# Reordering the prologue of an mLSTM + mixture-of-experts kernel: chunk 0's decays spread by fp32 products, two scans and a split moved

## The chip, the cores and the metric

The kernel runs on one core of one Trainium2 chip. The metric is the device time of one execution in microseconds (us), the median of three. A core has TensorE (PE in the rows; PEld is its weight load), VectorE (DVE), ScalarE (ACT), GpSimd (POOL) and SyncE (SP), which here only issues DMAs. Each engine takes its instructions in the order in which they were written; an instruction that has to wait holds back everything behind it on its engine.

## The reference

Two stages. The first is an mLSTM recurrence for 2 batches x 8 heads over 768 steps with head size 40:

```python
m_new  = max(f_gate + m, i_gate)
f_stab = exp(f_gate + m - m_new);  i_stab = exp(i_gate - m_new);  m = m_new
C = f_stab * C + i_stab * outer(v, k);   n = f_stab * n + i_stab * k
y[t] = sigmoid(o_gate) * (C @ q) / max(|n . q|, 1)
```

The second takes the 1536 tokens x of 320 numbers through all of four experts and adds them up with normalised weights p:

```python
out += p[:, e] * (relu(x @ w1[e]) @ w2[e])      # w1: 320 x 1024, w2: 1024 x 320
```

## The kernel before

The recurrence is computed in 12 chunks of 128 steps (`NCH`), six for each batch. For chunk n these helpers are called, each a few instructions:

- `spread(n)` copies the row of decays of each of the 8 heads to all 128 partitions, by 8 matrix products whose stationary operand is one column of a selector, broadcast (tile `fb`, in PSUM). `decay(n)` scans each of them against an identity on VectorE into a 128 x 128 matrix of products of decays (tile `dd`).
- `scores(n)` is k·q per head (tile `s`), `weigh(n)` multiplies it by `dd` (tile `pm`), `values(n)` scales v by the input gate (tile `vp`: a product on GpSimd and one column on ScalarE), `keys(n)` scales k (tile `kp`, GpSimd).
- `intra(n)` is pm·vp (tile `y`); `inter(n)` is q times the carried state (also a tile `y`), scaled on ScalarE into `yb`; `state(n)` makes the chunk's own state from kp and vp (tile `st`) and adds it to the decayed old one (tile `cs`); `carry(n)` decays the old state on GpSimd (tile `cd`).
- `norm(n)` divides and gates on VectorE (tile `xr`). `turn(n)` transposes `xr` on TensorE (tile `px`) and ScalarE writes the rounded part of x (tile `xst`); `turn_lo(n)` writes the remainder on VectorE.

The gates of the chunks of all 16 (batch, head) pairs are handled together, in two groups: columns of chunks 0 and 1 first, chunks 2 to 5 later (`(0, 2)` and `(2, NC)`). `gate_max` scans the running maximum, `gate_f` and `gate_i` make the decays `fs` and the input gates, `gate_starts` puts zeros at chunk starts, `gate_pair` splits the decays into two fp32r parts (tile `fr`) that `spread` reads, `gate_b` scans the running decays (VectorE, L248) and ScalarE copies them into `ib` (L252), `gate_t` transposes `ib` (tile `pit`, then `ibT`, L273), `gate_last` and `gate_l` make the per-chunk decay `bl` of the state.

The experts work on x and w1 in fp32r parts: `split_hi` on ScalarE rounds (tile `w1s`, L86), `split_lo` on GpSimd subtracts (L89). Expert 0's w1 is split in four quarters of 256 hidden columns (`quarter_hi`, `quarter_lo`). Expert 0 runs by `steps(k)` between the chunks: one step makes 256 hidden columns for 256 tokens in 16 products (tile `ph`, L128). The first step needs x of chunks 0 and 1 and quarter 0, the second needs quarter 1. Experts 1 to 3 follow when the recurrence is done.

All of this is under `manual_schedule`: the order of the calls is the order on every engine. Lines 489 to 583 are the prologue, written out by hand: the first DMAs, the gates, chunks 0 and 1, and the start of chunk 2. From line 595 a loop goes over chunks 2 to 11. `keep_warm(n)` is a product of zeros of n columns that fills a wait of TensorE (tile `pwm`). Tiles named `ph` and `po` take turns in two PSUM buffers each, and so do the tiles of `ps_w` and `ps_y`.

The lines that the prediction's steps touch, in the prologue of before:

```python
        gate_starts(0, 2, nc.vector)
        gate_pair(0, 2, nc.vector)
        gate_b(0, 2)
        gate_max(2, NC)
        spread(0, ps_h, "ph")
...
        norm(0)
...
        gate_b(2, NC)
        intra(1)
        norm(1)
...
        quarter_hi(1)
        gate_last(2, NC)
        quarter_lo(1)
```

Of the kernel before, what the change touches and what calls it, by code (L numbers as in the profile page):

```python
# [18 lines left out]
L = 128  # L19
# [22 lines left out]
def tile_mlstm_moe(ctx, tc, gt, qk, vk, ot, dp, w1, w2, out):  # L42
# [21 lines left out]
    def keep_warm(n, pool=ps_h, tag="ph"):  # L64

        pwm = pool.tile([L, n], F32, tag=tag, name="pwm")
        nc.tensor.matmul(pwm, zero[:, 0:L], zero[:, 0:n], start=True, stop=True)
# [96 lines left out]
    with ExitStack() as actx:  # L164
# [17 lines left out]
        def load_w1(half):  # L182
            f = slice(half * FF // 2, (half + 1) * FF // 2)
            wa = hps[0].tile([L, 2, FF // 2], F32, tag="h", name="wa")
            nc.sync.dma_start(wa, w1[0, :, 0:2, f])
            wb = hps[0].tile([L, 2, FF // 2], F32, tag="h", name="wb")
            nc.sync.dma_start(wb[:, 0], w1[0, :, 2, f])
            for i in range(2):
                w1r[2 * half + i] = wa[:, :, i * G:(i + 1) * G], wb[:, 0, i * G:(i + 1) * G]
# [9 lines left out]
        BH = B * H  # L199
        gat = gp.tile([BH, 2, S], F32, name="gat")  # L200
        mb = gp.tile([BH, S + 1], F32, name="mb")
        fs = gp.tile([BH, S], F32, name="fs")
        bs = gp.tile([BH, NC, L], F32, name="bs")

        ib = gp.tile([48, S], F32, name="ib")
# [15 lines left out]
        def gate_max(c0, c1):  # L221
            g = slice(c0 * L, c1 * L)
            nc.vector.tensor_tensor_scan(
                out=mb[:, c0 * L + 1:c1 * L + 1], data0=gat[:, 0, g], data1=gat[:, 1, g],
                initial=-1e30 if c0 == 0 else mb[:, c0 * L:c0 * L + 1],
                op0=ALU.add, op1=ALU.max,
            )
# [7 lines left out]
        def gate_starts(c0, c1, eng):  # L235

            eng.tensor_copy(bs[:, c0:c1, 0:1], fc[:, c0:c1, 0:1])
            eng.memset(fc[:, c0:c1, 0:1], 0.0)
# [15 lines left out]
        def gate_pair(c0, c1, eng):  # L254

            g = slice(c0 * L, c1 * L)
            eng.tensor_copy(fr[0:BH, g], fs[:, g])
            eng.tensor_sub(fr[32:32 + BH, g], fs[:, g], fr[0:BH, g].bitcast(F32))
# [18 lines left out]
        def gate_last(c0, c1):  # L277
            n, m = c1 - c0, B * NP
            last = lasts[c0] = gp.tile([BH, m, n], F32, tag=f"last{c0}", name="last")
            nc.gpsimd.tensor_mul(  # L280
                last, pair.unsqueeze(2).to_broadcast([BH, m, n]),
                gat[:, 0].rearrange("p (c t) -> p c t", t=L)[:, c0:c1, L - 1].unsqueeze(1)
                .to_broadcast([BH, m, n]),
            )
# [42 lines left out]
        def gate_o(j):  # L327
            og = acc[:, 2 * j:2 * j + 2]
            nc.scalar.activation(og, og, AF.Sigmoid)
# [4 lines left out]
        def spread(n, pool, tag):  # L334

            b, c = n // NC, n % NC
            fbs[n] = [pool.tile([L, 4, L], F32, tag=tag, name="fb") for _ in range(2)]
            for h in range(H):
                nc.tensor.matmul(
                    fbs[n][h // 4][:, h % 4, :],  # L340
                    sel[:, b * H + h:b * H + h + 1].to_broadcast([48, L]),
                    fr[:, c * L:(c + 1) * L], start=True, stop=True,
                )

        def load_f(n):
# [31 lines left out]
        def scores(n, pool=ps_w, tag="w"):  # L377
            ss[n] = [pool.tile([L, NP, L], F32, tag=tag, name="s") for _ in range(2)]
            qg, kg = qT(n), kT(n)
            for p in range(NP):  # L380
                for r in range(2):
                    q = slice(64 * r, 64 + D * r)
                    nc.tensor.matmul(ss[n][r][:, p, :], kg[q, p], qg[q, p], start=True, stop=True)  # L383
# [115 lines left out]
            load_vk(1, c)  # L499
        load_o(1)  # L500
        load_w1(1)
        make_identity(nc, ident)
        nc.gpsimd.memset(ib, 0.0)
        for t in vp + kp:
# [16 lines left out]
        gate_f(0, 2, nc.vector)  # L521
        gate_i(0, 2, nc.vector)
        gate_starts(0, 2, nc.vector)
        gate_pair(0, 2, nc.vector)
        gate_b(0, 2)
        gate_max(2, NC)
        spread(0, ps_h, "ph")
        scores(0)
        spread(1, ps_o, "po")
        gate_o(0)  # L530
        gate_last(0, 2)
        gate_f(2, NC, nc.gpsimd)
        gate_t(0, 2)
        keep_warm(512, ps_y, "y")
        decay(0)
        values(0)
        keys(0)
        weigh(0)
        scores(1, ps_h, "ph")
        gate_l(0, 2)  # L540
        gate_i(2, NC, nc.gpsimd)
        decay(1)
        intra(0)
        state(0, ps_w, "w")
        values(1)
        keys(1)
        weigh(1)
        keep_warm(256, ps_w, "w")
        inter(1, ps_w, "w")
        norm(0)  # L550
        gate_starts(2, NC, nc.gpsimd)
        gate_pair(2, NPE, nc.gpsimd)
        nc.sync.dma_start(f_d, fs)
        w2r = raws.tile([L, NF, DM], F32, tag="raw", name="w2r")
        nc.sync.dma_start(w2r, w2[0])
        carry(1)
        quarter_hi(0)
        quarter_lo(0)
        gate_b(2, NC)
        intra(1)  # L560
        norm(1)
        turn(0, ps_h, "ph")
        turn_lo(0)
        spread(2, ps_o, "po")
        keep_warm(256, ps_w, "w")
        turn(1, ps_h, "ph")
        turn_lo(1)
        scores(2)
        state(1)
        quarter_hi(1)  # L570
        gate_last(2, NC)
        quarter_lo(1)
# [174 lines left out]
```

## Time and profile before

| What | Value |
|---|---|
| Median of 3 runs | 430.84 us (430.82 to 430.94) |
| The profiled execution's own time | 431.67 us |
| Its span in the trace | 428.8 us |
| TensorE busy | 421.1 us (98%) |
| VectorE busy | 180.1 us (42%) |
| ScalarE busy | 125.7 us (29%) |
| GpSimd busy | 82.3 us (19%) |
| Granted TensorE clock | 1.00 in every stretch of 10 us |

Times in the rows are us from the start of the span. A timeline row gives the start, the length, the engine, the line, the operation, the tile written and the tiles read, and how many instructions stand together; in brackets the engine's idle time before it and what ended that. An fp32 product stands as two records on TensorE, an fp32r product or a transpose as one; a record's length holds the time in which the result runs out of the array, so that records overlap.

### The profile page before, as it was taken

The page shows a single profiled execution, that of the slowest core. Times are in us where ns is not written, and L with a number is a line of the kernel's source. Part 1 is how long each engine was busy: PE and PEld are TensorE (multiplying, and loading weights), DVE is VectorE, ACT ScalarE, POOL GpSimd, SP SyncE. Part 2 cuts the span into 40 slices and gives each one's busy share as a digit, 9 for nine tenths or more (in the row PEclk, how much of TensorE's full clock was granted, in tenths as well). Part 3 has the DMA queues.
Part 4 walks back from the last instruction along what each step waited for, and adds up shares of the span by engine and source line. Part 5 has one row for each costly group of instructions (what it writes and reads, how often), then busy time and mean ns, then how long its engine had stood idle before and what let it go on. Part 6 is the DMA issues. An engine that isn't in the chain of part 4 may idle for free.

```text
span 428.8 us, 6587 instructions
## 1 busy us (share of the span) xinstructions
PE 421.1 (98%) x2754; PEld 386.2 (90%) x2754; DVE 180.1 (42%) x321; ACT 125.7 (29%) x298; POOL 82.3 (19%) x94
## 2 busy tenths in 40 slices
PE   8999999999999999999999999999999999999997
PEld 5799899999998998898898998988989989889896
DVE  8869947574766321513313224223132242231321
ACT  5666233334324252403403114025031140120210
POOL 6854601220210260300710002007100010000000
PEclk9999999999999999999999999999999999999999
DMA  7985716347100011300110003001200000001001
GB/s 209 281 276 159 197 51 166 104 111 256 53 2 2 0 52 72 139 11 0 61 63 0 2 0 148 0 2 40 85 0 2 0 0 32 31 2 46 18 15 46
DMA packets 15077, 29.29 MB, mean 68 GB/s; under 512 B 1000, under 2 KB 10728, under 8 KB 13736
## 3 DMA queue, kind: packets, MB, share of 16 engines
q1 hardware_dynamic: 15048, 28.88, 21.9%
q8 instruction: 21, 0.34, 0.3%
q14 instruction: 8, 0.07, 0.1%
HBM read 26.86 MB, written 2.02 MB: 67 GB/s over the span
## 4 chain that ended last, share of the span: by engine, by line
PE 91%; DVE 4%; DMA 2%; issue 1%; ACT 1%; SPq 0%; POOL 0%; DVEq 0%
PE ph L128 41%; PE po L149 13%; PE po L150 13%; PE po L151 13%; PE y L445 5%; PE s L383 2%; PE y L431 2%; PE st L398 2%; DMA acc<-in_ot 2%; PE px L471 1%; DVE y L457 0%; DVE xr L461 0%; DVE w2s L89 0%; DVE xr L464 0%; DVE dd L356 0%
## 5 line engine op out<-in xcount | busy, mean ns | idle before, releaser
L128 PE MATMUL ph<-xst,w1s 128*128 128x512 f32 (+1 forms) x960 | 184.5, 350 | 0.0
L128 PEld LDWEIGHTS ph<-xst,w1s 128*128 128x128 f32 x960 | 154.8, 189 | 25.0
L137 ACT ACTIVATE h<-ph 128x512 fp32r<-128x512 f32 x96 | 57.4, 598 | 214.0 <-PE ph L128 213.9
L149 PE MATMUL po<-w2s,h 128*128 128x320 f32 x384 | 119.5, 311 | 0.0
L150 PE MATMUL po<-w2s,h 128*128 128x320 f32 x384 | 118.6, 309 | 0.0
L151 PE MATMUL po<-w2s,h 128*128 128x320 f32 x384 | 118.6, 309 | 0.0
L138 DVE SCALAR_TENSOR_TENSOR h<-ph,h 128x512 fp32r<-128x512 f32 x96 | 66.2, 690 | 121.4 <-ACT h L137 121.4
L149 PEld LDWEIGHTS po<-w2s,h 128*128 128x128 f32 x384 | 72.1, 188 | 0.9
L150 PEld LDWEIGHTS po<-w2s,h 128*128 128x128 f32 x384 | 72.1, 188 | 0.4
L151 PEld LDWEIGHTS po<-w2s,h 128*128 128x128 f32 x384 | 72.1, 188 | 0.0
L156 DVE SCALAR_TENSOR_TENSOR acc<-po,pw,acc 128x320 f32<-128x320 f32 x36 | 19.8, 551 | 100.0 <-PE po L151 100.0
L89 POOL TENSOR_TENSOR w1s<-raw,w1s 128x512 fp32r<-128x512 f32 (+1 forms) x24 | 23.6, 1011 | 62.4 <-ACT w1s L86 62.4
L356 DVE TENSOR_TENSOR_SCAN dd<-fb,id 128x512 f32<-128x512 f32 x24 | 29.3, 1264 | 0.2
L89 POOL TENSOR_TENSOR w2s<-raw,w2s 128x640 fp32r<-128x640 f32 x6 | 9.4, 1569 | 104.1 <-ACT w2s L86 104.1
L445 PE MATMUL y<-vp,pm 128*128 128x64 f32 x192 | 23.1, 273 | 1.2 <-DVE xst L479 0.9
L445 PEld LDWEIGHTS y<-vp,pm 128*128 128x128 f32 x192 | 22.5, 192 | 1.6 <-issue 1.1
L154 ACT ACTIVATE acc<-po,pw 128x320 f32<-128x320 f32 x12 | 6.3, 528 | 43.7 <-PE po L151 43.7
L438 ACT ACTIVATE yb<-y,ibT 128x41 f32<-128x41 f32 x80 | 16.0, 312 | 4.1 <-PE y L431 4.1
L389 DVE TENSOR_TENSOR pm<-s,dd 128x512 f32<-128x512 f32 x24 | 15.4, 683 | 0.5 <-PE s L383 0.3
L372 POOL TENSOR_TENSOR kp<-vk,dd 128x320 f32<-128x320 f32 x10 | 7.4, 736 | 36.6 <-DVE dd L356 36.6
L383 PE MATMUL s<-qk 64*128 64x128 f32 (+1 forms) x192 | 14.1, 284 | 0.0
L383 PEld LDWEIGHTS s<-qk 64*128 64x128 f32 (+1 forms) x192 | 11.8, 187 | 1.9 <-DVE dd L356 0.8
(89 smaller groups left out, 222.0 us busy)
## 6 DMA issues: line engine op xcount, KB each, us to landing
raw<-in_w SPq DMA_DIRECT2D x3, 1536.0 KB, 6.3
fb<-f_d SPq DMA_DIRECT2D x8, 512.0 KB, 7.5
raw<-in_w SPq DMA_DIRECT2D x3, 1280.0 KB
qk<-in_qk SPq DMA_DIRECT2D x4, 832.0 KB
vk<-in_vk SPq DMA_DIRECT2D x4, 640.0 KB, 8.1
acc<-in_ot SPq DMA_DIRECT2D x6, 320.0 KB, 10.8
out<-acc SPq DMA_DIRECT2D x12, 160.0 KB, 1.8
qk<-in_qk SPq DMA_DIRECT2D x4, 416.0 KB
```

Source lines behind the costliest of these rows:

```text
L89: eng.tensor_sub(lo, raw, hi.bitcast(F32))
L128: nc.tensor.matmul(ph[:, i, :], self.w1s[:, wi, f * L:(f + 1) * L], xst[:, xi, self.t0:self.t0 + n], start=(k == 0), stop=(k == len(TERMS) ...
L137: nc.scalar.activation(hh, ph, AF.Relu)
L138: nc.vector.scalar_tensor_tensor(out=hl, in0=ph, scalar=0.0, in1=hh.bitcast(F32), op0=ALU.max, op1=ALU.subtract)
L149: nc.tensor.matmul(po, hh[:, sl], ws[:, LO, f, :], start=(f == 0), stop=False)
L150: nc.tensor.matmul(po, hh[:, sl], ws[:, HI, f, :], start=False, stop=False)
L151: nc.tensor.matmul(po, hl[:, sl], ws[:, HI, f, :], start=False, stop=(f == NF - 1))
L156: nc.vector.scalar_tensor_tensor(out=acc[:, i, :], in0=po, scalar=pw[:, i, e:e + 1], in1=acc[:, i, :], op0=ALU.mult, op1=ALU.add,)
L356: nc.vector.tensor_tensor_scan(out=dds[n][:, 4 * i:4 * i + 4].rearrange("p h t -> p (h t)"), data0=fbs[n][i].rearrange("p h t -> p (h t)") ...
L383: nc.tensor.matmul(ss[n][r][:, p, :], kg[q, p], qg[q, p], start=True, stop=True)
L438: nc.scalar.activation(yb[:, h], y1[:, h, 0:D + 1], AF.Copy, scale=ibT[:, c, i:i + 1])
L445: nc.tensor.matmul(y[:, h, :], pms[n][:, h, :], vvs[n][:, h, :], start=True, stop=True)
```

## The change

Six things are edited, all in the prologue.

- The decays `fs` get a tile of 128 partitions (`fsw`), whose first 128 columns are cleared by a new memset on VectorE. Chunk 0's `spread` reads it directly, as fp32 products over 128 rows with a column of the identity. The other chunks read `fr` as before.
- `gate_pair` for chunk 0 goes; for chunk 1 it moves from VectorE to GpSimd.
- `gate_t(0, 2)`, and with it the copy to `ibT`, stands before the sigmoid of the output gates and the exponential of the later decays.
- `state(0)` stands before `intra(0)`, `values(1)` before the input gates of chunks 2 to 5, `intra(1)` before `norm(0)`, and `carry(1)` before the later `gate_starts` and `gate_pair`.
- `gate_b(2, NC)` moves from between `norm(0)` and `norm(1)` to behind `state(1)`.
- `scores(2)` stands before `turn(1)`, `spread(2)` behind it, and of the three `keep_warm` calls of this stretch one is left, in front of `turn(1)`.

```diff
-        fs = gp.tile([BH, S], F32, name="fs")
+        fsw = gp.tile([L, S], F32, name="fsw")
+        fs = fsw[0:BH]
...
-                    sel[:, b * H + h:b * H + h + 1].to_broadcast([48, L]),
-                    fr[:, c * L:(c + 1) * L], start=True, stop=True,
+                    ident[:, h:h + 1].to_broadcast([L, L]) if n == 0
+                    else sel[:, b * H + h:b * H + h + 1].to_broadcast([48, L]),
+                    (fsw if n == 0 else fr)[:, c * L:(c + 1) * L], start=True, stop=True,
...
+        nc.vector.memset(fsw[:, 0:L], 0.0)
...
-        gate_pair(0, 2, nc.vector)
         gate_b(0, 2)
         gate_max(2, NC)
+        gate_pair(1, 2, nc.gpsimd)
         spread(0, ps_h, "ph")
+        gate_t(0, 2)
         scores(0)
         spread(1, ps_o, "po")
+        gate_last(0, 2)
         gate_o(0)
-        gate_last(0, 2)
+        decay(0)
         gate_f(2, NC, nc.gpsimd)
-        gate_t(0, 2)
-        keep_warm(512, ps_y, "y")
-        decay(0)
...
+        decay(1)
+        values(1)
         gate_i(2, NC, nc.gpsimd)
-        decay(1)
+        state(0, ps_w, "w")
         intra(0)
-        state(0, ps_w, "w")
-        values(1)
...
-        keep_warm(256, ps_w, "w")
         inter(1, ps_w, "w")
+        intra(1)
         norm(0)
+        carry(1)
...
-        carry(1)
         quarter_hi(0)
         quarter_lo(0)
-        gate_b(2, NC)
-        intra(1)
         norm(1)
         turn(0, ps_h, "ph")
         turn_lo(0)
-        spread(2, ps_o, "po")
-        keep_warm(256, ps_w, "w")
+        scores(2)
+        keep_warm(256, ps_o, "po")
         turn(1, ps_h, "ph")
         turn_lo(1)
-        scores(2)
+        spread(2, ps_o, "po")
         state(1)
+        gate_b(2, NC)
         quarter_hi(1)
         gate_last(2, NC)
         quarter_lo(1)
```

What this does to the order on the engines is shown at three places. On ScalarE, early in the prologue, before: L273 is the copy to `ibT`, L329 the sigmoid, the second table load and L233 the exponential of the later decays, L368 the column of `vp`, L74 the copy of the first state.

```order
L252 ACTIVATE ib<-gat 16x256
L329 ACT_TABLE_LOAD
L329 ACTIVATE acc<-acc 128x640
L233 ACT_TABLE_LOAD
L233 ACTIVATE fs<-fs 16x512
L273 ACTIVATE ibT<-pit 128x96
L368 ACTIVATE vp_124<-ibT 128x8
L295 ACTIVATE bl<-pit 128x16
L243 ACTIVATE ib<-ib 16x512
L74 ACTIVATE cs_129<-st 64x4x64
```

The same place on ScalarE in the changed kernel, whose lines are two or three higher:

```order
L254 ACTIVATE ib<-gat 16x256
L275 ACTIVATE ibT<-pit 128x96
L331 ACT_TABLE_LOAD
L331 ACTIVATE acc<-acc 128x640
L235 ACT_TABLE_LOAD
L235 ACTIVATE fsw<-fsw 16x512
L371 ACTIVATE vp_124<-ibT 128x8
L297 ACTIVATE bl<-pit 128x16
L371 ACTIVATE vp_125<-ibT 128x8
L245 ACTIVATE ib<-ib 16x512
L74 ACTIVATE cs_129<-st 64x4x64
```

The copy to `ibT` moved ahead of both table loads; the column of `vp` stayed behind them, and the second chunk's column went ahead of the exponential of the later input gates.

On VectorE, around the end of chunk 1, before: L248 is the scan of the later running decays, L457 to L464 are `norm(1)`, L478 and L479 the remainders of x, L413 the sum of the state, L356 the decay scans of chunk 2.

```order
L464 TENSOR_TENSOR xr<-xr,y_254 128x320
L248 SCALAR_TENSOR_TENSOR gat<-fs,bs 16x512
L457 TENSOR_TENSOR y_314<-y_314,yb 128x8x41
...
L478 TENSOR_TENSOR xst<-px,xst 128x2x128
L479 TENSOR_TENSOR xst<-px,xst 64x128
L413 TENSOR_TENSOR cs_128<-cd,st 64x4x64
L413 TENSOR_TENSOR cs_128<-cd,st 40x4x41
L356 SCALAR_TENSOR_TENSOR dd<-fb,id_117 128x512 x2
```

The same place on VectorE in the changed kernel:

```order
L467 TENSOR_TENSOR xr<-xr,y_262 128x320
L460 TENSOR_TENSOR y_289<-y_289,yb 128x8x41
...
L481 TENSOR_TENSOR xst<-px,xst 128x2x128
L482 TENSOR_TENSOR xst<-px,xst 64x128
L416 TENSOR_TENSOR cs_128<-cd,st 64x4x64
L416 TENSOR_TENSOR cs_128<-cd,st 40x4x41
L250 SCALAR_TENSOR_TENSOR gat<-fsw,bs 16x512
L359 SCALAR_TENSOR_TENSOR dd<-fb,id_117 128x512 x2
```

The scan now stands behind both additions of the state of chunk 1.

On ScalarE, what follows that scan, before: L252 copies it into `ib`, L473 and L474 write x, L86 rounds quarter 1 of w1, then the next sigmoid with its table load and the first evacuation of an expert's step.

```order
L252 ACTIVATE ib<-gat 16x512
L473 ACTIVATE xst<-px 128x2x128
L474 ACTIVATE xst<-px 64x128
L473 ACTIVATE xst<-px 128x2x128
L474 ACTIVATE xst<-px 64x128
L86 ACTIVATE w1s_91<-wa 128x2x256
L86 ACTIVATE w1s_91<-wb 128x256
L329 ACT_TABLE_LOAD
L329 ACTIVATE acc<-acc 128x640
L137 ACTIVATE h<-ph 128x512
```

The same place in the changed kernel:

```order
L476 ACTIVATE xst<-px 128x2x128
L477 ACTIVATE xst<-px 64x128
L476 ACTIVATE xst<-px 128x2x128
L477 ACTIVATE xst<-px 64x128
L254 ACTIVATE ib<-gat 16x512
L86 ACTIVATE w1s_91<-wa 128x2x256
L86 ACTIVATE w1s_91<-wb 128x256
L331 ACT_TABLE_LOAD
L331 ACTIVATE acc<-acc 128x640
L137 ACTIVATE h<-ph 128x512
```

The copy of the running decays went behind x of both chunks, and stands directly ahead of the rounding of quarter 1 of w1.

## Rows read from the trace of the kernel before

**Rows 1.** The first line of the page: the span.

```profile
span 428.8 us, 6587 instructions
```

**Rows 2.** The chain of waits that ended last, from chunk 2 to the transposes of chunk 3; columns: start, us, engine, tile, line.

```profile
31.65 1.77 PE y L445 x14
...
34.30 0.41 DVE cs L413
...
48.48 0.50 DVE xr L464
...
49.11 0.52 PE px L471 x3
```

**Rows 3.** The timeline of VectorE in the prologue and at chunk 4's decays (start us, us, engine, line, operation, out<-in, idle before).

```profile
0.94 0.48 DVE L507 MEMSET fr<- 48x512 f32 x1
...
5.68 0.06 DVE L238 MEMSET fs<- 16x2 f32 x1
...
6.54 0.68 DVE L248 TENSOR_TENSOR_SCAN gat<-fs,bs 16x256 f32<-16x256 f32 x1
7.14 1.25 DVE L223 TENSOR_TENSOR_SCAN mb<-gat,mb 16x512 f32<-16x512 f32 x1
8.32 2.30 DVE L356 TENSOR_TENSOR_SCAN dd<-fb,id 128x512 f32<-128x512 f32 x2
...
17.03 1.33 DVE L248 TENSOR_TENSOR_SCAN gat<-fs,bs 16x512 f32<-16x512 f32 x1
19.24 0.51 DVE L457 TENSOR_TENSOR y<-y,yb 128x328 f32<-128x328 f32 x1 [0.88 <-PE y L445]
...
24.04 0.76 DVE L413 TENSOR_TENSOR cs<-cd,st 64x256 f32<-64x256 f32 x2 [0.76 <-PE st L398]
24.81 2.34 DVE L356 TENSOR_TENSOR_SCAN dd<-fb,id 128x512 f32<-128x512 f32 x2
...
30.31 1.28 DVE L389 TENSOR_TENSOR pm<-s,dd 128x512 f32<-128x512 f32 x2
...
41.94 3.67 DVE L356 TENSOR_TENSOR_SCAN dd<-fb,id 128x512 f32<-128x512 f32 x2
```

**Rows 4.** The timeline of TensorE in the prologue, same columns.

```profile
6.65 0.96 PE L339 MATMUL fb<-fr,sel 48*128 48x128 f32 x7 [0.71 <-DVE fr L258]
...
12.69 2.00 PE L445 MATMUL y<-vp,pm 128*128 128x64 f32 x16 [0.22 <-POOL vp L367]
14.52 0.93 PE L398 MATMUL st<-vp,kp 128*104 128x105 f32 x8
...
16.24 1.16 PE L431 MATMUL y<-cs,qk 104*128 104x128 f32 x8 [0.33 <-ACT cs L74]
...
21.38 0.55 PE L471 MATMUL px<-ident,xr 128*128 128x128 f32 x3 [0.26 <-DVE xr L464]
...
23.70 2.15 PE L128 MATMUL ph<-xst,w1s 128*128 128x256 f32 x16
25.78 1.09 PE L269 MATMUL pit<-ident,ib 48*128 48x48 f32 x8
26.80 2.18 PE L128 MATMUL ph<-xst,w1s 128*128 128x256 f32 x16
```

**Rows 5.** The timeline of ScalarE in the prologue, same columns.

```profile
7.68 1.28 ACT L329 ACT_TABLE_LOAD   x1
9.02 0.74 ACT L329 ACTIVATE acc<-acc 128x640 f32<-128x640 f32 x1
...
11.07 0.63 ACT L233 ACTIVATE fs<-fs 16x512 f32<-16x512 f32 x1
11.61 0.22 ACT L273 ACTIVATE ibT<-pit 128x96 f32<-128x96 f32 x1
...
15.49 0.70 ACT L74 ACTIVATE cs<-st 64x256 f32<-64x256 f32 x2 [0.46 <-PE st L398]
...
19.88 0.63 ACT L252 ACTIVATE ib<-gat 16x512 f32<-16x512 f32 x1
...
22.40 0.62 ACT L86 ACTIVATE w1s<-wa 128x512 fp32r<-128x512 f32 x1
...
29.07 0.60 ACT L137 ACTIVATE h<-ph 128x512 fp32r<-128x512 f32 x1 [1.59 <-PE ph L128]
```

**Rows 6.** The timeline of GpSimd in the prologue and at chunk 4's decays, same columns.

```profile
7.30 1.10 POOL L280 TENSOR_TENSOR last<-pair,gat 16x16 f32<-16x16 f32 x1 [2.45 <-DVE gat L248]
...
9.82 1.08 POOL L232 TENSOR_TENSOR fs<-fs,mb 16x512 f32<-16x512 f32 x1
11.91 0.72 POOL L367 TENSOR_TENSOR vp<-vk,ibT 128x320 f32<-128x320 f32 x1 [1.01 <-ACT ibT L273]
12.59 0.74 POOL L372 TENSOR_TENSOR kp<-vk,dd 128x320 f32<-128x320 f32 x1
13.28 1.08 POOL L242 TENSOR_TENSOR ib<-gat,mb 16x512 f32<-16x512 f32 x1
...
21.55 0.25 POOL L280 TENSOR_TENSOR last<-pair,gat 16x32 f32<-16x32 f32 x1
23.10 1.27 POOL L89 TENSOR_TENSOR w1s<-wa,w1s 128x512 fp32r<-128x512 f32 x1 [1.30 <-ACT w1s L86]
...
42.98 3.98 POOL L89 TENSOR_TENSOR w2s<-w2r,w2s 128x640 fp32r<-128x640 f32 x2 [4.98 <-ACT w2s L86]
```

## The prediction

> **What bounds the kernel now.** I read the page first: a span of 428.8 us [rows 1], TensorE busy for 98% of it. That alone would say that only TensorE's own work counts, so I then read the chain of waits for the stretch behind the prologue. From 34.30, where the state of chunk 2 is added, to 48.98, where `norm(3)` ends, its pieces are VectorE's, one behind the other; TensorE takes over at 49.11 with the transposes of chunk 3 and keeps the chain from there [rows 2]. So the prologue counts through one event only: when VectorE can start that run at 34.30. It starts after `st` of chunk 2, which stands on TensorE behind `intra(2)`, whose second product starts at 31.65 [rows 2], just after the two `pm` of chunk 2 (30.31 + 1.28 = 31.59) [rows 3]. These stand behind the remainder of the second expert step, which waits for ScalarE's h at 29.07, which waits for TensorE's second step [rows 5], begun at 26.80 [rows 4]. Whatever moves the second step's end moves the end of the kernel by as much.
>
> Then the timelines, engine by engine. Up to the transposes of chunk 1 at 21.38 TensorE waits for others four times [rows 4]; from 23.70 to the second step's start at 26.80 it goes without a wait [rows 4]. What the second step needs was early: quarter 1 of w1 was there at 23.10 + 1.27 = 24.37 [rows 6], and the copy of the running decays for `pit` at 19.88 + 0.63 [rows 5].
>
> **The head, up to the transposes of chunk 1.** The new memset has 128 columns; one of 512 took 0.48, one of 16x2 took 0.06 [rows 3]. I take 0.2, between them. `gate_pair` leaves VectorE: from the end of the memset at 5.74 to the scan at 6.54 [rows 3] 0.80 goes, less the 0.04 that remain. Net, VectorE's scans come about 0.55 earlier: `gate_b` at 5.98, `gate_max` at 6.6, `dd` at 7.75 instead of 8.32.
>
> TensorE can start the spread at 6.1 instead of 6.65. The fp32 form gives 16 records. Sixteen fp32 records of 64 columns over 128 rows took 1.83 from start to next start (12.69 to 14.52); eight of 128 columns took 1.16 with the run-out, so twice that, 2.32, is the upper end [rows 4]. I take 1.83, since the record's own pace was the same in both. It ends at 7.93; `pit` follows (half of 1.09, [rows 4]), and `ibT` is copied at 8.5 to 8.75.
>
> Here the ScalarE order bites. Before, the first table load started at 7.68 and `ibT` came last, at 11.61 [rows 5]. Now the loads start at 8.75: 1.28 + 0.74 + 1.28 + 0.63 [rows 5] lead to 12.7, and the `vp` column behind them (I give it the 0.22 of `ibT`) to 12.9. Chunk 0's first `st` cannot start before that; before, the product in this place started at 12.69 [rows 4]. So hoisting `ibT` gains nothing at this point and loses 0.25. The two switches go by the rows: from the sigmoid's end (9.76) to the exponential (11.07) is 1.31, load included [rows 5]. The Trainium skill (ScalarE: Activation LUTs, What ACT_TABLE_LOAD costs) gives an additional drain of about 1.38 us for a switch, 2.66 in all; by that the `vp` column would come some 2.8 later and the sum below would be near +3.5, but the trace shows no such drain, and the measurement decides.
>
> `st` (0.8, its 0.93 without the run-out) and `y` (1.83) then occupy TensorE to 15.6. `inter(1)` needs the state's copy on ScalarE, which stands behind the exponential of the later input gates, which waits for GpSimd. GpSimd now has the pair of chunk 1, two small instructions, ready at 6.0, just when VectorE starts `gate_b` and then `gate_max`. The row of `last` shows what such a meeting costs: 1.10 at 7.30, against 0.25 at 21.55 for one of twice the size, ending as `gate_max` ended (8.39) [rows 3, 6]. So I let the pair finish at 8.4 and `last` at 8.7, 0.3 later than before. From there 2.5 to the end of the second `fs` instruction (8.40 to 10.90), then `vp`, `kp`, `vp` and the later input gates, 0.72 + 0.74 + 0.72 + 1.08 [rows 6], end at 14.4; exponential and copy, 0.63 + 0.70 [rows 5], give 15.7. `inter(1)` starts at 15.7 instead of 16.24, 0.55 earlier. The fp32 products' upper end would put `y`'s end and `inter(1)` at 16.1, 0.15 earlier; without the meeting 15.6, 0.65 earlier. That the meeting is a full block is also the Trainium skill's rule (SBUF — State Buffer, Who interferes with whom): a VectorE instruction with two inputs in SBUF and a GpSimd instruction that reads SBUF exclude each other, and the later one waits to the end. The `last` row agrees with it.
>
> From `inter(1)` everything to the transposes is TensorE, ScalarE and VectorE in the same sequence; `norm(0)` ends about 17.2, and since the scan at 17.03 (1.33, [rows 3]) has gone from its back, `norm(1)` waits for TensorE alone, as before (0.88 idle at 19.24, [rows 3]). So the transposes of chunk 1 come at 21.38 - 0.55 = 20.8. Behind them the order has `spread(2)` where `scores(2)` was: both eight products of about 1 us, a draw. First expert step: 23.70 - 0.55 = 23.15; VectorE's addition of the state: 24.04 - 0.55 = 23.5.
>
> **The late scan.** Here the order takes it back. The addition ends its turn after 0.77 (24.04 to 24.81, [rows 3]), at 24.25. Then `gate_b(2, NC)`: 1.33 [rows 3], to 25.6. ScalarE has stood at its copy since x of chunk 1 and everything behind waits too: copy 0.63, to 26.25; rounding quarter 1, 0.62 [rows 5], to 26.8 (they overlap by a little). GpSimd subtracts: 1.27 [rows 6], to 28.1. On TensorE the first step ends its turn 2.08 after its start (23.70 to 25.78, [rows 4]), at 25.2, and `pit` waits for the copy until 26.3, a new wait of 1.05; `pit` takes 1.02 (25.78 to 26.80), the second step's first product goes at 27.3, and its second needs GpSimd's remainder and starts at 28.1, a new wait of 0.6. Before, that second product followed directly behind 26.80, at about 27.0. The step ends 1.1 later than before: that is the sum, -0.55 for the head and +1.65 for the late scan.
>
> Then h at 30.2, `pm` of chunk 2 at 31.4, the addition at 35.4 instead of 34.30, and VectorE's run to the transposes, which come at 50.2. The new waits on VectorE's side have no cover, as rows 2 show; TensorE's spare time before 49.11 only grows. SP's queue: the store of the decays and the weights behind it start about 1 us later, since `carry(1)` stands ahead of them on GpSimd; what they bring is used from 38 on, so I cost that at nothing. The left-out warm-up products cost nothing as long as the granted clock stays at 1.00.
>
> Against the profiled execution: 431.67 + 1.1 = 432.8. The runs' median is 430.84, 0.83 below it; the difference is carried over: 431.9.
>
> **The rivals.**
> *The late scan is covered.* If the second step does not in fact wait for the copy, the rounding and the remainder, the head's gain goes through: 430.84 - 0.55 = 430.3. For it: TensorE is 98% busy and before it never waited there. Against it: the new order on ScalarE, and 1.33 + 0.63 + 0.62 + 1.27 behind an addition that itself stands behind TensorE's `st`.
>
> *The meeting at chunk 4 goes the other way.* The second scan of chunk 4's decays meets the two `w2s` instructions of GpSimd: the two scans took 3.67 at 41.94 where two undisturbed ones took 2.34, and GpSimd began at 42.98 [rows 3, 6], just before the second scan (41.94 and half of 2.34 is 43.1). If GpSimd comes 0.1 to 0.2 later in relation to VectorE, the scan is first, and 3.67 - 2.34 = 1.33 of VectorE's run goes: +1.1 - 1.33, 430.6, not slower. Both sides hang on `st` and `intra` of chunk 2 and should move alike, but the margin is small. It decides from the point where the second scan starts ahead of GpSimd.
>
> *The fp32 products run at the lower clock.* Left-out warm-ups and new waits of about a microsecond on TensorE could let the granted clock fall from 2.4 to 1.2 GHz. The spread would take up to twice 1.83, and the head some 1.3 to 2 more than I have: about 433.5. Against it: the wait of 0.71 at 6.65 [rows 4] left the clock at 1.00.
>
> **How the numbers follow.** Forecast as worked out: 0.57. Late scan covered: 0.12. Chunk 4 the other way: 0.20. Lower clock or another added wait: 0.11. A measurement of this kernel tells 0.2% from no change, that is 0.86 us: slower means above 431.70, faster below 429.98. The forecast's own range is 431.2 (head at its best, and 0.4 for overlaps that I added as if in series) to 432.6 (fp32 upper end); three quarters of it, 0.43, lie above 431.70, 0.14 inside. Chunk 4: 0.15 inside, 0.05 faster. Covered: 0.07 inside, 0.05 faster. Lower clock: 0.11 slower. Together: faster 0.10, same 0.36, slower 0.54. The range reaches down to the two rivals on the other side and up to the fp32 bound: 430.1 to 432.7.
>
> **What would show it.** In the profile of the changed kernel: `dd` of chunk 0 near 7.75; the first `st` near 12.9, released by ScalarE's `vp` column; the transposes of chunk 1 near 20.8; the scan of the later decays near 24.3; a wait of TensorE of about 1.05 before `pit`, released by ScalarE, and a second of 0.6 in the second step, released by GpSimd; the transposes of chunk 3 near 50.2. I am wrong if the second expert step starts before 26.8 without a wait, if the scans of chunk 4 take 2.3 instead of 3.7, or if the granted clock leaves 1.00.

## The result and the profile after

| | before | changed |
|---|---|---|
| Median, both measured together | 430.89 us | 442.31 us |
| Its executions | 430.82, 430.84, 430.94, 433.81 | 434.05, 439.99, 444.63, 445.33 |
| Granted TensorE clock, mean of each of these executions of the changed kernel | | 0.992, 0.977, 0.961, 0.965 |
| Profiled execution | 431.67 (span 428.8) | 445.33 (span 443.5) |

The changed kernel is slower: by the medians 442.31 - 430.89 = 11.4 us, and the ratio is 1.0133 with an interval of 1.0083 to 1.0182. Every ratio in this document leaves out executions more than 1.5% above the fastest of their kernel, here the two above 444 us, which are the same effect at a larger size, as the clock beside each time shows. So this ratio rests on two executions only. The forecast was 431.9 within 430.1 to 432.7: the sign came out, the size did not.

The first thing to look at is the clock. The page's first line, the share of the engines and the row of the granted clock, in tenths over 40 slices of the span:

```profile
span 443.5 us, 6596 instructions
...
PE 435.0 (98%) x2758; PEld 399.9 (90%) x2758; DVE 179.9 (41%) x320; ACT 125.2 (28%) x298; POOL 82.5 (19%) x96
...
PEclk9658799999999999999999999999999999999999
```

TensorE is busy for 98% as before, and for 435.0 us instead of 421.1. A busy share tells nothing of how fast the work went. The clock row does: slices two to five are at 5 to 8, where before had 9 throughout. Cut into stretches at the places where the clock changes (length, then busy time of PE, PEld, DVE, ACT and POOL, the granted clock, the DMA share, GB/s):

```profile
13.30:33.80 20.50, 19.68 (x96) 18.31 (x97) 8.26 (x21) 5.58 (x21) 5.52 (x9) 0.50 0.54 175
33.80:37.20 3.40, 2.62 (x20) 2.16 (x18) 2.92 (x3) 2.74 (x4) 1.67 (x3) 1.00 0.36 101
37.20:40.60 3.40, 3.40 (x16) 3.18 (x16) 0.69 (x1) 1.77 (x5) 1.96 (x3) 0.50 1.01 256
40.60:44.00 3.40, 3.38 (x28) 3.13 (x27) 2.66 (x4) 2.38 (x9) 2.53 (x3) 1.00 1.00 259
44.00:50.85 6.85, 6.85 (x41) 6.44 (x41) 4.66 (x11) 1.65 (x7) 4.74 (x6) 0.50 0.37 118
50.85:440.00 389.15, 386.91 (x2497) 358.73 (x2495) 148.82 (x260) 104.07 (x244) 54.88 (x54) 1.00 0.16 50
```

1.00 is 2.4 GHz and 0.50 is 1.2 GHz. The clock was at the lower level for 20.5 + 3.4 + 6.85 = 30.75 us. At half speed that can cost up to half of it, 15.4; the span is 443.5 - 428.8 = 14.7 longer than before's. The transposes of chunk 3 come behind all of this; they are the first of these rows (the second, the scans of chunk 4's decays, is used further down):

```profile
63.76 0.52 PE L474 MATMUL px<-ident,xr 128*128 128x128 f32 x3 [0.94 <-DVE xr L467]
56.54 3.70 DVE L359 TENSOR_TENSOR_SCAN dd<-fb,id 128x512 f32<-128x512 f32 x2
```

The transposes are 63.76 - 49.11 = 14.65 later than in before [rows 2], so behind them nothing more is lost. The experiment that holds the clock up, below, puts 12.2 of the 14.7 down to the falls.

What happened at the falls stands in the timeline of TensorE, which answers to [rows 4]:

```profile
0.78 6.50 PE L67 MATMUL pwm<-const-float32-0.0 128*128 128x512 f32 x8 [0.78 <-PEq L730]
7.12 1.95 PE L341 MATMUL fb<-fsw,ident 128*128 128x128 f32 x16
...
14.12 1.70 PE L401 MATMUL st<-vp,kp 128*104 128x105 f32 x8 [1.42 <-POOL ib L244]
15.61 3.55 PE L448 MATMUL y<-vp,pm 128*128 128x64 f32 x16
...
31.97 2.95 PE L128 MATMUL ph<-xst,w1s 128*128 128x256 f32 x16
35.10 1.09 PE L271 MATMUL pit<-ident,ib 48*128 48x48 f32 x8 [0.18 <-ACT ib L254]
...
37.11 3.51 PE L128 MATMUL ph<-xst,w1s 128*128 128x256 f32 x15 [0.60 <-POOL w1s L89]
```

The first fall, at 13.3, lies inside the wait of 1.42 ahead of chunk 0's `st`. From there the products take nearly twice as long: `y` 3.55 against 2.00 [rows 4]. The second, at 37.2, follows the wait of 0.60 in the second expert step. The third, at 44.0, follows no wait: TensorE was busy for 3.38 of the 3.40 us before it. The first rows also show that the spread started at 7.12, behind warm-up products that ran until 7.28.

VectorE, ScalarE and GpSimd, which answer to [rows 3], [rows 5] and [rows 6], in this order:

```profile
5.92 0.68 DVE L250 TENSOR_TENSOR_SCAN gat<-fsw,bs 16x256 f32<-16x256 f32 x1
6.53 1.25 DVE L225 TENSOR_TENSOR_SCAN mb<-gat,mb 16x512 f32<-16x512 f32 x1
8.21 2.34 DVE L359 TENSOR_TENSOR_SCAN dd<-fb,id 128x512 f32<-128x512 f32 x2 [0.43 <-PE fb L341]
```

```profile
9.68 0.25 ACT L275 ACTIVATE ibT<-pit 128x96 f32<-128x96 f32 x1 [2.63 <-PE pit L271]
9.95 1.28 ACT L331 ACT_TABLE_LOAD   x1
11.24 0.74 ACT L331 ACTIVATE acc<-acc 128x640 f32<-128x640 f32 x1
11.99 1.28 ACT L235 ACT_TABLE_LOAD   x1
13.29 0.63 ACT L235 ACTIVATE fsw<-fsw 16x512 f32<-16x512 f32 x1
13.83 0.20 ACT L371 ACTIVATE vp<-ibT 128x8 f32<-128x8 f32 x1
```

```profile
6.03 0.66 POOL L259 CAST fr<-fsw 16x128 fp32r<-16x128 f32 x1 [1.17 <-ACT ib L245]
6.77 1.25 POOL L260 TENSOR_TENSOR fr<-fsw,fr 16x128 fp32r<-16x128 f32 x1
...
12.71 1.08 POOL L244 TENSOR_TENSOR ib<-gat,mb 16x512 f32<-16x512 f32 x1
```

GpSimd's two small instructions took 0.66 and 1.25 while VectorE's two scans stood beside them; the same two on twice the columns took 0.39 and 0.71 at 18.01 and 18.48 of this trace, while VectorE was idle. The wait of 1.42 is put down to GpSimd's `ib`, which ended at 12.71 + 1.08 = 13.79; ScalarE's `vp` column at 13.83 + 0.20 = 14.03 came later, behind the two table loads, and `st` reads that column and not `ib`. That is the release that the prediction named, 1.2 us later than it said.

### The profile page after: what moved, and what is told of

Same layout as the page of the kernel before. It is cut to its first block, busy times and chain, and to the rows that moved or that the text cites. A ratio compares the mean times of both kernels' runs of the same rounds, so it can differ in the third digit from the quotient of the medians.

```text
span 443.5 us, 6596 instructions
## 1 busy us (share of the span) xinstructions
PE 435.0 (98%) x2758; PEld 399.9 (90%) x2758; DVE 179.9 (41%) x320; ACT 125.2 (28%) x298; POOL 82.5 (19%) x96
## 4 chain that ended last, share of the span: by engine, by line
PE 92%; DVE 4%; POOL 2%; issue 1%; ACT 1%; DVEq 0%; POOLq 0%; ACTq 0%
PE ph L128 40%; PE po L149 13%; PE po L150 12%; PE po L151 12%; PE y L448 5%; PE s L386 3%; PE st L401 2%; PE y L434 2%; PE px L474 1%; PE fb L341 1%; DVE w2s L89 0%; DVE dd L359 0%; POOL vp L370 0%; POOL w1s L89 0%; POOL fr L260 0%
## 5 line engine op out<-in xcount | busy, mean ns | idle before, releaser
L128 PE MATMUL ph<-xst,w1s 128*128 128x512 f32 (+1 forms) x960 | 187.7, 354 | 0.6 <-POOL w1s L89 0.6
L128 PEld LDWEIGHTS ph<-xst,w1s 128*128 128x128 f32 x960 | 157.8, 193 | 25.9 <-POOL w1s L89 0.8
L448 PE MATMUL y<-vp,pm 128*128 128x64 f32 x192 | 27.1, 302 | 0.9 <-DVE xst L482 0.9
L448 PEld LDWEIGHTS y<-vp,pm 128*128 128x128 f32 x192 | 26.6, 221 | 1.2 <-issue 1.1
L386 PE MATMUL s<-qk 64*128 64x128 f32 (+1 forms) x192 | 16.1, 310 | 0.0
L392 DVE TENSOR_TENSOR pm<-s,dd 128x512 f32<-128x512 f32 x24 | 15.4, 682 | 0.5 <-PE s L386 0.3
L386 PEld LDWEIGHTS s<-qk 64*128 64x128 f32 (+1 forms) x192 | 13.6, 210 | 1.3 <-PE px L474 0.4
```

The costliest lines, as they stand in the source:

```text
L128: nc.tensor.matmul(ph[:, i, :], self.w1s[:, wi, f * L:(f + 1) * L], xst[:, xi, self.t0:self.t0 + n], start=(k == 0), stop=(k == len(TERMS) ...
L448: nc.tensor.matmul(y[:, h, :], pms[n][:, h, :], vvs[n][:, h, :], start=True, stop=True)
```

## The experiments

Two theories were to be told apart. One: the two products of zeros that were left out of the head kept the clock up, and their absence alone brings the fall. The other: the waits of the late scan bring it. Each run's ratio is against executions of before on the same chip.

**The zeros put back, the late scan kept.** They stand ahead of `scores(1)` and `state(0)`, where the changed kernel waited, and not at their old places.

```diff
         weigh(0)
+        keep_warm(512, ps_y, "y")
         scores(1, ps_h, "ph")
...
         gate_i(2, NC, nc.gpsimd)
+        keep_warm(256, ps_w, "w")
         state(0, ps_w, "w")
```

> The changed kernel with the two left-out warm-up products put back, 512 columns ahead of scores(1) and 256 ahead of state(0), where TensorE waited 1.42 us in the trace of the changed kernel. Theory A (the fallen clock is the loss, and the missing work of TensorE in the head let it fall): the granted clock stays at 1.00 or close to it in most runs and the time falls from about 440 to 431.5 to 433. Theory B (the late scan and its waits are the loss, and the clock fell because of them): the time stays at 434 to 445, with granted clocks of 0.96 to 0.99 as in the changed kernel.

Measured: 439.92 us (433.69 to 439.93), ratio 1.0162 (1.0087 to 1.0238). The head was mended: the clock stood at 1.00 from 6.0 to 29.9. Then it fell all the same (windows, columns as above, and the timeline of TensorE):

```profile
6.00:29.90 23.90, 22.22 (x189) 19.08 (x188) 17.95 (x30) 12.93 (x31) 14.79 (x20) 1.00 0.85 267
29.90:47.00 17.10, 17.10 (x87) 16.29 (x86) 8.72 (x16) 5.07 (x20) 8.72 (x10) 0.50 0.50 136
```

```profile
27.05 1.09 PE L271 MATMUL pit<-ident,ib 48*128 48x48 f32 x8 [0.89 <-ACT ib L254]
...
29.04 2.91 PE L128 MATMUL ph<-xst,w1s 128*128 128x256 f32 x15 [0.59 <-POOL w1s L89]
...
147.50 1.97 PE L448 MATMUL y<-vp,pm 128*128 128x64 f32 x16 [0.91 <-DVE xst L482]
```

The two waits are the ones forecast (1.05 and 0.6), released by the engines forecast, and the fall follows the second. So the head alone is not the cause.

**The scan put back between the two norms, no zeros added.**

```diff
         quarter_lo(0)
+        gate_b(2, NC)
         norm(1)
...
         state(1)
-        gate_b(2, NC)
         quarter_hi(1)
```

> The changed kernel with the scan of the later running decays, gate_b(2, NC), back between norm(0) and norm(1); no warm-up product is put back. Theory A (missing work of TensorE in the head): the clock falls as before, since in the trace of the changed kernel it fell at 13.3 us, before any wait for that scan; 433 to 444. Theory B (the late scan): the clock stays at 1.00 and the time is 430 to 431.

Measured: 439.41 us (438.61 to 439.90), ratio 1.0185 (1.0145 to 1.0224). The clock was at 0.50 from 15.2 to 32.2, after a wait of 1.33 ahead of `st` (its window, and TensorE's rows of the spread and of `st`):

```profile
15.20:32.20 17.00, 17.00 (x84) 15.60 (x84) 8.12 (x20) 6.96 (x19) 6.40 (x10) 0.50 0.93 276
```

```profile
6.35 1.83 PE L341 MATMUL fb<-fsw,ident 128*128 128x128 f32 x15
...
13.35 0.95 PE L401 MATMUL st<-vp,kp 128*104 128x105 f32 x8 [1.33 <-POOL vp L370]
```

So the late scan alone is not the cause either.

**Before, without two of its products of zeros.**

```diff
-        keep_warm(512, ps_y, "y")
         decay(0)
...
-        keep_warm(256, ps_w, "w")
         inter(1, ps_w, "w")
```

> The kernel before without its warm-up products of 512 columns ahead of decay(0) and of 256 columns ahead of inter(1); everything else as before. Theory A: these two alone hold the clock, so that it falls in some runs and the time is 433 or more in those. If the fp32 spread or the new order of the head is what lets it fall, the clock stays at 1.00 here and the time is within 0.3 us of 430.9.

Measured: 438.10 us (437.75 to 442.16), ratio 1.0178 (1.0120 to 1.0236). Of the change only left-out zeros are in this kernel, and it loses 438.10 - 430.70 = 7.4 us by the medians. The window of the fall and the wait that ends at it; TensorE had also waited 0.80 ahead of the spread, at 6.65:

```profile
10.40:30.90 20.50, 19.64 (x99) 17.76 (x99) 10.88 (x23) 8.89 (x27) 9.92 (x15) 0.50 0.97 286
```

```profile
10.47 2.27 PE L383 MATMUL s<-qk 64*128 64x128 f32 x16 [0.53 <-DMA qk<-in_qk]
```

**Both mended: the zeros of the first experiment and the scan of the second.**

```diff
         weigh(0)
+        keep_warm(512, ps_y, "y")
         scores(1, ps_h, "ph")
...
+        keep_warm(256, ps_w, "w")
         state(0, ps_w, "w")
...
         quarter_lo(0)
+        gate_b(2, NC)
         norm(1)
...
         state(1)
-        gate_b(2, NC)
         quarter_hi(1)
```

> Both: the two warm-up products put back and the scan back between norm(0) and norm(1). At a granted clock of 1.00 this leaves the head's part of the change alone, which I put at 0.55 us earlier: 430.3, and the difference to the kernel with the warm-up products only is the price of the late scan, which I put at 1.65 us. If the late scan is covered, the two differ by less than 0.3 us.

Measured: 430.76 us (430.18 to 431.19, ten executions, all at 0.996 or 1.00), ratio 0.9989 (0.9971 to 1.0006): equal to before. It differs from the first experiment by the scan alone and from the second by the zeros alone, and only with both does the loss go. This settles that there are two causes, each enough by itself. It also gives what the head is worth at the full clock:

```profile
7.07 1.95 PE L341 MATMUL fb<-fsw,ident 128*128 128x128 f32 x16
...
21.90 0.55 PE L474 MATMUL px<-ident,xr 128*128 128x128 f32 x3 [0.20 <-DVE xr L467]
...
27.27 2.18 PE L128 MATMUL ph<-xst,w1s 128*128 128x256 f32 x16
```

The transposes of chunk 1 stand at 21.90, and the second step at 27.27 without a wait; before had 21.38 and 26.80 [rows 4], so in this execution, the longest of the ten, nothing came earlier.

**The late scan at the full clock.** To the first experiment two products of zeros are added where its waits were:

```diff
         steps(1)
+        fill = ps_y.tile([L, 512], F32, tag="y", name="pwm")
+        nc.tensor.matmul(fill, zero[:, 0:L], zero[:, 0:512], start=True, stop=True)
         gate_t(2, NC)
         values(2)
+        nc.tensor.matmul(fill[:, 0:256], zero[:, 0:L], zero[:, 0:256], start=True, stop=True)
         steps(1)
```

> The changed kernel with the two warm-up products put back, and two more products of zeros (512 columns ahead of pit of the later chunks, 256 ahead of the second expert step) in the two waits that the late scan makes. Theory C (the late scan lets the clock fall through its waits, and costs 1.1 to 1.7 us by itself): the clock stays at 1.00, the time is 432.0 to 432.6, and against the kernel with the scan moved back it is 1.3 to 1.9 us longer. If the late scan let the clock fall in another way than by these waits, it falls here too: 434 to 440.

Measured: 432.37 us (431.91 to 433.03, ten executions, all at 1.00), ratio 1.0027 (1.0015 to 1.0038). By the medians this is 432.37 - 431.18 = 1.2 us above before on its chip, where the first experiment was 439.92 - 430.70 = 9.2 above before on another: the two products took away some 8 us and left the lateness (the last row is that of chunk 3's transposes):

```profile
26.25 1.02 PE L581 MATMUL pwm<-const-float32-0.0 128*128 128x512 f32 x2
27.31 1.09 PE L271 MATMUL pit<-ident,ib 48*128 48x48 f32 x8
28.32 0.70 PE L584 MATMUL pwm<-const-float32-0.0 128*128 128x256 f32 x2
...
29.31 2.06 PE L128 MATMUL ph<-xst,w1s 128*128 128x256 f32 x15 [0.17 <-POOL w1s L89]
...
51.53 0.52 PE L474 MATMUL px<-ident,xr 128*128 128x128 f32 x3 [0.96 <-DVE xr L467]
```

The fills took no time of their own: `pit` and the second step's second product are 0.26 and 0.27 later than in the first experiment, and so was the spread (7.16 against 6.89). The transposes of chunk 3 come 63.76 - 51.53 = 12.2 earlier than in the changed kernel, and the span is 12.2 shorter: that is what the falls cost in the profiled execution.

Against the kernel with both mended it is 432.37 - 430.76 = 1.6 us: the price of the late scan with the clock held. The two stood on different chips; by their ratios it is (1.0027 - 0.9989) x 431 = 1.6 as well, with intervals that leave it open by 0.9 either way; by the medians, each above its own before, it is 1.1. In the traces, from the transposes of chunk 1 to those of chunk 3, it is 29.5 (21.99 to 51.53) against 27.7 (21.90 to 49.60), 1.8.

**Before, with the scan moved and nothing else.**

```diff
         quarter_lo(0)
-        gate_b(2, NC)
         intra(1)
...
         state(1)
+        gate_b(2, NC)
         quarter_hi(1)
```

> The kernel before with one edit: the scan of the later running decays moved from in front of intra(1) to behind state(1). All warm-up products stay. Theory C: two new waits of TensorE (0.9 to 1.1 us ahead of pit, 0.6 in the second step) as in the changed kernel with warm-ups, the granted clock falls behind them in most runs, and the time is 433 to 440. If the clock stays at 1.00: 432.0 to 432.6. If the late scan is harmless alone: 430.5 to 431.

Measured: 439.33 us (434.12 to 439.67), ratio 1.0150 (1.0092 to 1.0208). Waits of 0.87 and 0.60 at the two places, and a clock of 0.50 from 29.2 to 42.9:

```profile
29.20:42.90 13.70, 13.70 (x71) 13.01 (x70) 6.07 (x9) 5.42 (x19) 8.22 (x11) 0.50 0.64 175
```

```profile
26.69 1.09 PE L269 MATMUL pit<-ident,ib 48*128 48x48 f32 x8 [0.87 <-ACT ib L252]
...
28.70 3.16 PE L128 MATMUL ph<-xst,w1s 128*128 128x256 f32 x15 [0.60 <-POOL w1s L89]
```

The one moved line brings 439.33 - 431.18 = 8.2 us by the medians, beside 11.4 for the whole change. The left-out zeros alone brought 7.4, so the two losses don't add up.

**The fp32 spread, the memset and the pair on GpSimd, and nothing else.** Beside the first hunks of the change (the tile `fsw`, the products of `spread` and the memset) it holds:

```diff
         gate_starts(0, 2, nc.vector)
-        gate_pair(0, 2, nc.vector)
         gate_b(0, 2)
         gate_max(2, NC)
+        gate_pair(1, 2, nc.gpsimd)
```

> The kernel before with the first part of the change alone: decays of chunk 0 spread by fp32 products, the memset, and the pair of chunk 1 on GpSimd; order and warm-up products otherwise as before. Theory A and C have no part in this: the clock stays at 1.00, dd of chunk 0 starts 0.2 to 0.6 us earlier, ScalarE's copy to ibT still stands behind the table loads, and the time is within 0.4 us of the kernel before. If the fp32 products themselves disturb the clock, it falls: 433 or more.

Measured: 431.90 us (431.10 to 435.70), ratio 1.0029 (0.9999 to 1.0058). The five executions at 1.00 lie at 431.1 to 431.5, the two at 0.999 at 432.32 and 432.35, and the three at 0.984 to 0.988 at 434.8 to 435.7; before had none below 0.996 in the 19 beside them. The spread starts at 7.29 and takes 1.95, where in the trace of before it started at 6.65 and took about 1.0:

```profile
7.29 1.95 PE L340 MATMUL fb<-fsw,ident 128*128 128x128 f32 x16
```

No gain, and a clock that falls in some executions.

**Before, without one product of zeros at a time.** First the 512 columns, then, in another kernel, the 256 ahead of `inter(1)`:

```diff
         gate_t(0, 2)
-        keep_warm(512, ps_y, "y")
         decay(0)
```

```diff
         weigh(1)
-        keep_warm(256, ps_w, "w")
         inter(1, ps_w, "w")
```

> The kernel before without its product of 512 zero columns ahead of decay(0) alone. In the trace without both products the clock fell at 10.4 us, at the end of a wait of 0.53 us for the second chunk's q and k, which that product had filled. If that wait is what counts: the clock falls here in most runs, 434 to 442. If it takes both: 430.5 to 431.5.

> The kernel before without its product of 256 zero columns ahead of inter(1) alone. The wait that it shortens was 0.33 us with it and should be 0.75 to 0.8 without. If a wait of this size is enough by itself: the clock falls in some runs, 433 to 440. If only the earlier one counts: 430.5 to 431.5 in all.

Without the 512: 433.32 us (432.04 to 444.14), ratio 1.0049 (1.0031 to 1.0068) from the three shortest, and all five executions were below 1.00 (0.996 to 0.965). Without the 256: 431.09 us (430.49 to 434.91), ratio 1.0006 (0.9971 to 1.0040), with two of ten executions below 1.00, at 0.988 and 0.984. Of before's 14 in that set five were below 1.00: three at 0.996 and one each at 0.987 and 0.984. So of the zeros left out of the head, each taken out alone, only the 512 columns count. Without both, all four executions took 437.75 or more, so that the 256 are not shown to be without effect where the 512 are gone. The trace without the 512 also shows the fp32r spread starting late, behind warm-up products that ended at 7.50:

```profile
7.44 0.99 PE L339 MATMUL fb<-fr,sel 48*128 48x128 f32 x7
```

**Three attempts at a faster order**, all on before's fp32r spread. In all three, `gate_t` and `values(0)` go ahead of the sigmoid, `state(0)` ahead of `intra(0)`, the later gates behind them, `intra(1)` ahead of `norm(0)`, and the 256 zero columns ahead of `inter(1)` are left out:

```diff
         spread(1, ps_o, "po")
+        gate_last(0, 2)
+        gate_t(0, 2)
+        values(0)
         gate_o(0)
-        gate_last(0, 2)
-        gate_f(2, NC, nc.gpsimd)
-        gate_t(0, 2)
         keep_warm(512, ps_y, "y")
...
+        state(0, ps_w, "w")
         intra(0)
-        state(0, ps_w, "w")
-        values(1)
+        gate_f(2, NC, nc.gpsimd)
...
-        keep_warm(256, ps_w, "w")
         inter(1, ps_w, "w")
+        intra(1)
         norm(0)
```

The first keeps the scan between the norms. The second puts it behind `spread(2)`, with zeros of 512 and 256 columns ahead of `turn(1)`; the third is the second with the 512 alone there:

```diff
         turn(0, ps_h, "ph")
+        scores(2)
+        keep_warm(512, ps_o, "po")
+        turn(1, ps_h, "ph")
+        spread(2, ps_o, "po")
+        gate_b(2, NC)
         turn_lo(0)
-        spread(2, ps_o, "po")
-        keep_warm(256, ps_w, "w")
-        turn(1, ps_h, "ph")
         turn_lo(1)
-        scores(2)
```

> A try at a faster order, from the kernel before: the column of vp right behind the copy to ibT and both ahead of the table loads; vp, kp and vp ahead of the exponential of the later decays; state(0) ahead of intra(0); the later input gates behind inter(1); the scan between norm(0) and norm(1); the product of 512 zero columns stays, that of 256 ahead of inter(1) goes, since I expect no wait there. If the head is worth what its waits of 0.22, 0.33 and 0.88 us say: norm(1) starts near 18.4 instead of 19.24, and the time is 429.8 to 430.2 at a clock of 1.00. If the missing 256 columns let the clock fall: 433 to 440.

> The tried order again, with what held it up removed: in its trace spread(2) waited 2.46 us for GpSimd's pair and the clock fell at 20.6. Now scores(2) and products of 512 and 256 zero columns fill the wait for norm(1), spread(2) stands behind turn(1), and the later running decays are scanned right behind norm(1), ahead of the remainders of x, which themselves wait for the transposes. If the late scan is harmless where it fits ahead of the remainders: clock 1.00 in most runs, norm(1) from about 18.6, first expert step near 23.1, time 429.9 to 430.4. If the scan there delays the first step or leaves new waits: 430.7 or more, and 433 or more with a fallen clock.

> The tried order once more, since the granted clock was 0.56 from its first rise on in most runs of the last try, before its order differs from before, so that they say nothing of it. The product of 256 zero columns ahead of turn(1) is left out, as that of 512 fills the wait. At a clock of 1.00: norm(1) near 18.6, first expert step near 23.2 instead of 23.70, 430.2 to 430.5 where before is 430.5 to 430.7. If a new wait is left somewhere, the clock falls in some runs and they take 432 or more; then the order is no gain, whatever its head is worth.

The first: 437.38 us (434.57 to 437.61), ratio 1.0111 (1.0074 to 1.0148). Its chunk 2 spread waited 2.46 us for GpSimd's `fr`, and the clock fell at 20.6 in that wait:

```profile
21.37 1.97 PE L339 MATMUL fb<-fr,sel 48*128 48x128 f32 x8 [2.46 <-POOL fr L258]
```

The second gave 702.79, 704.54, 516.61 and 433.14 us and is inconclusive (below). The third: 430.63 us (430.22 to 431.69), ratio 0.9992 (0.9977 to 1.0006), clock 0.996 to 1.00. In it TensorE is ahead of before up to the second step, as its timeline shows; the last row is VectorE's addition of chunk 2's state:

```profile
20.08 0.49 PE L471 MATMUL px<-ident,xr 128*128 128x128 f32 x3
...
26.02 2.18 PE L128 MATMUL ph<-xst,w1s 128*128 128x256 f32 x16
...
33.93 0.76 DVE L413 TENSOR_TENSOR cs<-cd,st 64x256 f32<-64x256 f32 x2 [0.88 <-PE st L398]
```

The transposes come 1.3 earlier and the second step 0.8 (21.38 and 26.80, [rows 4]), but the addition of chunk 2's state at 33.93 is only 0.4 earlier than 34.30 [rows 2], and the span 428.5 against 428.8 [rows 1]. VectorE was idle for 0.88 ahead of that addition, and `st`, which its row names, was done some 0.5 earlier, at 32.48 + 0.93; what held VectorE in between the profile doesn't show. No version here beats before by more than the measurement can tell.

## Why the prediction was wrong

**The clock: the step that failed.** "The left-out warm-up products cost nothing as long as the granted clock stays at 1.00" put the zeros at nothing, and the rival in which the clock doesn't stay got 0.11, at 433.5. It did not stay in any of the four executions (0.992 to 0.961), which the prediction had named as a sign of being wrong, and leaving out the zeros alone cost 7.4 us. Two errors lie in it. The rival was held unlikely because "the wait of 0.71 at 6.65 [rows 4] left the clock at 1.00"; that is one wait in one trace, and before without its two products of zeros fell at a wait of 0.53. And its price, "some 1.3 to 2 more", counted one stretch of the head; a fall lasted 20.5 us here, and the three falls of the profiled execution cost 12.2. The late scan's waits, worked out as 1.05 and 0.6, were costed at their own length; moved alone, the scan cost 8.2 us instead of 1.65.

**The late scan: right in kind and size.** Forecast +1.65, with a wait of 1.05 released by ScalarE and one of 0.6 released by GpSimd. With the head's clock held they were 0.89 and 0.59, and at the full clock the late scan costs 1.6 (1.1 to 1.8 by the other readings above). In the changed kernel's own trace the first wait is only 0.18, because there the first expert step, partly at the lower clock, took 2.95 instead of 2.15 [rows 4] and covered the rest. The rival that the late scan is covered is out.

**The head: too early in the traces, open in the times.** Forecast -0.55, with the spread at 6.1, `dd` at 7.75, the first `st` at 12.9, the transposes of chunk 1 at 20.8. Seen: 7.12, 8.21, 14.12; and with the clock held 21.90. VectorE was early as forecast (its scan at 5.92 against 5.98). What was missed is TensorE's own queue: the spread stands behind the warm-up products, and in every trace these end only after the clock has first risen. Their records took 1.06 us each ahead of the first rise and 0.59 behind it; the clock row and the windows count the time ahead of that rise as 1.00, so it has to be read from these lengths. The moment of the rise differs from execution to execution, and the warm-up products ended at 5.94 in the trace of before, 7.28 in that of the changed kernel, 7.50 in that of before without the 512 columns, and 6.51 in the second experiment. The spread followed them: fp32r 6.65 (where it still waited for VectorE) and 7.44, fp32 7.12 and 6.35. So the forecast measured from an execution in which the clock rose early, and with a late rise either form starts when the warm-up products end. The sixteen records themselves cost 1.88 from start to next start, close to the forecast 1.83, some 0.9 more than fp32r. By the times the head at the full clock, with the zeros back in it, is worth about 0: 430.76 against before's 430.70; the ratio 0.9989 with its interval leaves anything from 1.2 earlier to 0.3 later, which holds the forecast -0.55 too.

**ScalarE's order and the meeting on GpSimd: right.** From `ibT` to the end of the `vp` column it is 14.03 - 9.68 = 4.35, forecast 4.4; the sigmoid's end to the exponential is 13.29 - 11.98 = 1.31 again. So the trace disagrees once more with the additional drain that the Trainium skill (ScalarE: Activation LUTs, What ACT_TABLE_LOAD costs) gives. GpSimd's pair ended at 6.77 + 1.25 = 8.02, forecast 8.4, and the Trainium skill's rule of exclusion (SBUF — State Buffer, Who interferes with whom) agrees with the 0.66 and 1.25: they ended at 6.69 and 8.02, behind the scans' ends at 6.60 and 7.78.

**Chunk 4 the other way: no.** The two scans took 3.70 at 56.54 in the changed kernel and 3.67 with the clock held, as in before (3.67, [rows 3]).

**The sum at the full clock** was forecast as +1.1. The nearest kernel that holds the clock, with the zeros in both places, is at a ratio of 1.0027, which is +1.2 us of 431. That is the forecast's own case, so that the sign is not luck; that the sum agrees this closely partly is, as its head is open by more than its own size. It is not what the changed kernel does.

## What to carry to other kernels

Products of zeros are part of a tuned order: before one is left out, or a wait is opened on TensorE, ask what the clock does there, and price a fall by how long it lasts (3.4 to 20.5 us here) and not by the wait. Where a wait goes, look at what the engine's own queue does ahead of it, in more than one execution. And after any change read the row of the granted clock before any busy share.

## What the hardware showed that was not expected

Short waits can precede a long fall, and the length of the wait does not decide it. A wait of 0.53, with one of 0.80 some 4 us ahead of it, ended with the clock at 0.50 for 20.5 us; without the 512 columns it fell in another trace behind waits of 0.30 and 0.10; and at 44.0 in the changed kernel it fell with no wait ahead of it since 37.1. Yet 0.71 in before [rows 4] left it at 1.00. So that filling the two waits of the late scan keeps the clock up is shown, and that a wait as such brings a fall is not. The same wait went both ways: in the first experiment the 0.91 at 147.50 (shown above) was followed by 0.50 from 149.4 to 152.8, and in before the same product waited as long while the clock stayed at 1.00 to the end:

```profile
139.15 1.97 PE L445 MATMUL y<-vp,pm 128*128 128x64 f32 x16 [0.91 <-DVE xst L479]
```

Before itself was at 0.996 or less in 16 of the 63 executions that stood beside the experiments (0.984 at the lowest, 434.88 us). What decides between these cases is open.

Once down, the clock stayed down while TensorE was busy throughout: 17.10 of 17.10 us in the first experiment, 17.00 of 17.00 in the second.

A third level appeared once. In the second of the faster orders the granted clock rose from the start only to 0.56, changed between that and 0.50, and held 0.56 to the end (windows, columns as above):

```profile
5.90:9.20 3.30, 3.30 (x15) 1.86 (x13) 3.14 (x5) 0.42 (x1) 1.10 (x1) 0.56 1.03 283
...
235.00:700.00 465.00, 462.81 (x1595) 336.92 (x1593) 77.03 (x118) 65.14 (x116) 34.71 (x32) 0.56 0.05 20
```

Three of its four executions were like that or partly so, while before's executions in the same set held 0.984 to 1.00. At 5.8, where it rose, this kernel and before had run the same instructions, so the order is no explanation that the trace supports; the cause stays open, and the run says nothing of the order.
